# Retention ahead of two MLP layers on one core: output products grouped by tile shape, the last chunk widened to 128 tokens, and shared PSUM banks begun without zero products

## The chip, the cores and the metric

The kernel runs on one core of a Trainium2 chip. The metric is the device time in microseconds (us), here that of the one core. TensorE (PE in the profile) multiplies matrices into PSUM; VectorE (DVE), ScalarE (ACT) and GpSimd (POOL) work elementwise; SyncE (SP) issues most transfers. Each engine takes its instructions in a fixed order, so an instruction that waits holds up all that stand behind it on its engine.

## The reference

Retention (causal linear attention with a decay per head) is followed by two MLP layers. There are 4 batches, 8 heads, 576 tokens and 64 dimensions per head; the layers see 2304 tokens of 512 features and have 2048 hidden features.

```python
scores = scale * np.matmul(q, k.transpose(0, 1, 3, 2))
Dmat = np.where(rel >= 0, gamma[:, None, None] ** rel[None, :, :], 0.0)   # rel = i - j
attn_out = np.matmul(scores * Dmat, v)
x = attn_out.transpose(0, 2, 1, 3).reshape(2304, 512)
h = x @ moe_w_in;  x = np.maximum(0.01 * h, h) @ moe_w_out
h = x @ moe2_w_in; out = (h - np.tanh(h)) @ moe2_w_out
```

## The kernel before, in words

`retention()` goes through 16 pairs of heads (batch b, pair p), one pair per turn of its loop. The 576 tokens of a pair are four chunks of 128 (`NFULL`) and a last one of 64 (`TAIL`). Per pair the loop makes, in plain float32:

- `scores`: within each whole chunk, keys against queries (L393, one product per head and chunk, 64 rows of the array each), and the last chunk for both heads at once (L396, 64 stationary columns);
- `mask`: the causal mask and a decay factor on DVE (L406 for the whole chunks, L412 for the last), giving `pt`;
- `states_mm` and `states`: keys against values of each chunk (L424), from which ACT (L435) and DVE (L439) build the running state `st` at each chunk's end;
- `outputs_mm`, one pair later: for each chunk a "far" product of the state with the queries (L453, the full 128x128 array) and two "near" products of `pt` with the values (L458, 64 stationary columns for each head, in two halves of the array; for the last chunk 64 rows and 64 columns);
- `finish`: the outputs are split into a high part `xh` (ACT, L468) and a low part `xl` (DVE, L469), the last chunk first.

The queries and the values of the whole chunks are decayed in `prep` on POOL (L359, L364) one pair ahead, those of the last chunk in `prep_tail` on DVE (L372) and ACT (L382; L376 lays out its queries by head). Five transfers per pair are issued two pairs ahead by SP: queries, keys, `kn`, `vn`, and `vt` (the last chunk's values); each waits until the buffer it fills, one of three, is free.

From pair 5 on, each turn of the loop also has one step (the last turn two) of the first layer with 256 tokens: `h_mm` (L183, into `x_b`, 12 products of 256 columns in float32r, three for each of four slices, high and low parts), `act_a` and `chain` (L195, L217, L226, L227), and two steps later `o_mm` (L258, 12 products, into `a`). In the turns of pairs 0 to 8, DVE, ACT and POOL also turn the first weights from float64 bits into two float32r parts (`narrow_ops`, L126 to L147, and `split_piece`, L163 and L164); `fill` deals these steps out between the others. Where two outputs of 256 columns share a PSUM bank (`pack` is 2), `o_mm` first clears the bank with a product of one row of zeros (L243), 512 columns wide, and all others accumulate. This happens in six blocks: three in `retention`, and the block of 256 tokens of each of the other three groups of layer 1.

`layers()` does the rest of the two layers in steps of 512 tokens. The order on every engine is that in which the code is written (`manual_schedule`). The last chunk's scores `t_sc` and its output `o_tail` share the PSUM bank `x_a`; the far product into `o_tail` therefore stands behind the masking of `t_sc` (L412) of the pair that follows it.

Of the kernel before, what the change touches and what calls it, by code (L numbers as in the profile page):

```python
# [10 lines left out]
F32 = mybir.dt.float32  # L11
# [7 lines left out]
P = 128  # L19
CH = 128  # L20

# h - tanh(h) = tanh(h) * u * rho(u) with u = h^2 and rho(u) = (h / tanh(h) - 1) / u.
# For |h| <= TANH_T, rho(u) is RHO_C * (u - RHO_V)^2 + RHO_A to float32's accuracy.
# [4 lines left out]
# The float32 range, as the high words of float64 seen as float32.  # L28
# [5 lines left out]
def retention_moe_moe(  # L34
# [6 lines left out]
    vt: bass.AP,  # L41
# [32 lines left out]
    zero = keep.tile([P, 1], F32R, name="zero")  # L74

# [1 line left out]
    # Layer 1's first group takes QW tokens at a time while retention goes on.  # L77
# [33 lines left out]
    def narrow_ops(key):  # L111
        """The steps that make a float32 tile of a loaded piece."""
# [119 lines left out]
    def o_mm(s):  # L232
# [4 lines left out]
        if f == 0:  # L237
            ac_ps[s] = [
                pools["a"].tile([P, 512], F32, tag="a", name="a") for _ in range(cnt // pack)
            ]  # L240
            if pack > 1:
                for a in ac_ps[s]:
                    nc.tensor.matmul(  # L243
                        out=a, lhsT=zero[:1].to_broadcast([1, P]),
                        rhs=zero[:1].to_broadcast([1, 512]), start=True, stop=False,
                    )
        ps = ac_ps[s - f]
        gt, w = ga.pop(s), wt[m, 1, g * GF + f]
        for d in range(cnt):
# [3 lines left out]
            for i, (wi, gi) in enumerate(((0, 0), (0, 1), (1, 0))):  # L253
                if m == 0:
                    l, r = w[:, wi, ds], gt[:, gi, :n]
                else:
                    l, r = gt[:, gi, ds], w[:, wi, :]
                nc.tensor.matmul(  # L258
                    out=o, lhsT=l, rhs=r,
                    start=f == 0 and i == 0 and pack == 1,  # L260
                    stop=f == GF - 1 and i == 2 and (d + 1) % pack == 0,
                )
# [31 lines left out]
    def split_order(keys):  # L294
        """Pieces in the order in which the last block of a group lets go of their places."""
        return sorted(keys, key=lambda k: (k[2] + LAG * k[1], k[1]))

    def piece_ops(keys, split=True):
        """What the pieces take, in order: each is loaded two pieces ahead and split after
        the next one's first half."""  # L300
# [10 lines left out]
    def retention():  # L311
        with ExitStack() as ac:
# [8 lines left out]
            # The last chunk's scores of both heads and its output share a bank.  # L321
            x_a = ps_s.tile([P, 512], F32, name="x_a")
            x_b = ps_s.tile([P, 512], F32, name="x_b")
            t_sc = x_a[:TAIL, :2 * TAIL].rearrange("p (h r) -> p h r", h=2)
# [355 lines left out]
```

## Time and profile before

| | |
|---|---|
| median of 3 runs | 937.0 us (934.05 to 937.63) |
| span of the profiled execution | 935.3 us |
| median less that span | 1.7 us |
| PE busy | 906.2 us (97% of the span) |
| DVE, POOL, ACT busy | 595.9, 464.3, 397.6 us |

The profile is of one execution; no device time is listed for it beside its span, so the median is compared with the span. A busy PE is not a PE at its peak, because matmuls overlap: what a product costs is read from the start of one group to the start of the next. In the rows below a tile shape such as 128*64 is rows by columns of the array that a product uses. A float32 product has two entries, a float32r product one.

### The profile page before, as it was taken

Reading aid. Unit: us, or ns where it says so; the run is one execution under the profiler, and the core shown is the slowest. Engines: PE = TensorE matmul, PEld = TensorE weight load, DVE = VectorE, ACT = ScalarE, POOL = GpSimd, SP = SyncE. Lnnn points to the kernel's source line nnn. Section 1 sums busy time; section 2 is a strip of 40 time slices with the busy share of each in tenths; the row PEclk is TensorE's granted clock in tenths of the full one; section 3 lists DMA queues with packets and bytes.
Section 4 is the critical chain, followed back from the end, with each engine's and each line's share of the span. In section 5 each row is a group of like instructions: output and inputs, shape, how many; then the busy total and the mean of one; then the engine's idle time right before and its main releaser. Section 6 shows DMA issues by size and latency. Waiting matters only on the chain.

```text
span 935.3 us, 12947 instructions
## 1 busy us (share of the span) xinstructions
PE 906.2 (97%) x4844; PEld 737.5 (79%) x4844; DVE 595.9 (64%) x989; ACT 397.6 (43%) x809; POOL 464.3 (50%) x364
## 2 busy tenths in 40 slices
PE   4989999999999999999999999999999999999998
PEld 3667778888888888888888878888878877888886
DVE  5787554875555465527683677758886778754544
ACT  2443332224222322232333655576456545575454
POOL 3454421236222533245565855586457755595444
PEclk8999999999999999999999999999999999999999
DMA  7654340211111011101111011201120011001111
GB/s 233 224 178 154 103 141 13 78 68 46 46 68 46 0 46 68 68 1 46 46 52 39 3 46 66 69 1 45 46 68 23 23 45 68 1 1 46 45 46 68
DMA packets 22942, 57.78 MB, mean 62 GB/s; under 512 B 2784, under 2 KB 4192, under 8 KB 22880
## 3 DMA queue, kind: packets, MB, share of 16 engines
q1 hardware_dynamic: 22304, 56.63, 17.6%
q8 instruction: 38, 0.62, 0.3%
q10 hardware_dynamic: 576, 0.33, 0.1%
q14 instruction: 24, 0.20, 0.1%
HBM read 52.24 MB, written 4.72 MB: 61 GB/s over the span
## 4 chain that ended last, share of the span: by engine, by line
PE 70%; DVE 12%; POOL 9%; issue 4%; ACT 3%; DMA 2%; ACTq 0%; SPq 0%; DVEq 0%; POOLq 0%
PE a L258 32%; PE h L183 31%; POOL v L205 4%; POOL g L227 3%; DVE v L221 3%; DVE v L224 2%; DVE acc L282 2%; ACT g L226 2%; PE o L458 1%; PE x_b L183 1%; PE o L453 1%; DMA kv<-in_vt 1%; POOL wp L164 1%; PE sc L393 1%; DVE pt L406 1%
## 5 line engine op out<-in xcount | busy, mean ns | idle before, releaser
L183 PE MATMUL h<-xh,wp 128*128 128x512 f32 (+1 forms) x1216 | 374.7, 373 | 0.0
L183 PEld LDWEIGHTS h<-xh,wp 128*128 128x128 f32 x1216 | 222.0, 188 | 45.4
L183 PE MATMUL h<-xl,wp 128*128 128x512 f32 (+1 forms) x608 | 226.9, 373 | 0.0
L258 PE MATMUL a<-wp,g 128*128 128x512 f32 x864 | 212.9, 392 | 5.5 <-POOL g L227 5.3
L258 PE MATMUL a<-g,wp 128*128 128x512 f32 (+1 forms) x1008 | 214.2, 362 | 1.2 <-POOL g L227 1.2
L227 POOL TENSOR_TENSOR g<-a,g 128x512 fp32r<-128x512 f32 (+1 forms) x84 | 107.8, 1283 | 206.1 <-ACT g L226 194.7
L258 PEld LDWEIGHTS a<-g,wp 128*128 128x128 f32 x1008 | 171.4, 189 | 33.9 <-POOL g L227 1.4
L258 PEld LDWEIGHTS a<-wp,g 128*128 128x128 f32 x864 | 160.6, 188 | 43.9 <-POOL g L227 9.6
L227 POOL TENSOR_TENSOR g<-v,g 128x512 fp32r<-128x512 f32 (+1 forms) x80 | 103.9, 1298 | 142.1 <-ACT g L226 142.0
L183 PEld LDWEIGHTS h<-xl,wp 128*128 128x128 f32 x608 | 113.9, 187 | 22.6
L164 POOL TENSOR_TENSOR wp<-cw,wp 128x512 fp32r<-128x512 f32 x64 | 90.2, 1419 | 54.1 <-ACT wp L163 50.6
L147 DVE SCALAR_TENSOR_TENSOR cw<-st,cw 128x512 uint32<-128x512 uint32 x128 | 115.0, 898 | 3.0
L226 ACT ACTIVATE g<-v 128x512 fp32r<-128x512 f32 (+1 forms) x80 | 47.2, 590 | 163.4 <-DVE v L224 162.3
L195 ACT ACTIVATE a<-h 128x512 f32<-128x512 f32 (+1 forms) x72 | 40.5, 563 | 171.2 <-PE h L183 171.2
L217 DVE TENSOR_TENSOR a<-h,a 128x512 f32<-128x512 f32 (+1 forms) x72 | 46.3, 643 | 100.7 <-ACT a L195 100.6
L205 POOL TENSOR_TENSOR v<-t,u 128x512 f32<-128x512 f32 (+1 forms) x80 | 101.8, 1272 | 12.0 <-ACT t L204 11.9
L282 DVE TENSOR_TENSOR acc<-a,acc 128x512 f32<-128x512 f32 (+1 forms) x114 | 72.0, 659 | 51.5 <-PE a L258 51.5
L221 DVE SCALAR_TENSOR_TENSOR v<-q,v 128x512 f32<-128x512 f32 (+1 forms) x80 | 58.2, 728 | 59.1 <-POOL v L205 58.1
L220 DVE TENSOR_TENSOR h<-h,t 128x512 f32<-128x512 f32 (+1 forms) x80 | 51.2, 640 | 48.5 <-ACT t L204 48.5
L226 ACT ACTIVATE g<-a 128x512 fp32r<-128x512 f32 (+1 forms) x84 | 47.9, 570 | 80.2 <-DVE a L217 80.1
L141 DVE TENSOR_SCALAR cw<-cw 128x512 uint32<-128x512 uint32 x64 | 63.2, 988 | 1.5
L224 DVE COPY_PREDICATED v<-mk,h 128x512 f32<-128x512 uint32 (+1 forms) x80 | 54.9, 687 | 8.2
(60 smaller groups left out, 769.7 us busy)
## 6 DMA issues: line engine op xcount, KB each, us to landing
st<-in_w1i SPq DMA_DIRECT2D x16, 512.0 KB, 3.3
st<-in_w1o SPq DMA_DIRECT2D x16, 512.0 KB, 3.2
st<-in_w2i SPq DMA_DIRECT2D x16, 512.0 KB, 3.2
st<-in_w2o SPq DMA_DIRECT2D x16, 512.0 KB, 3.2
qk<-in_qT SPq DMA_DIRECT2D x16, 288.0 KB, 2.8
qk<-in_kT SPq DMA_DIRECT2D x16, 288.0 KB, 3.4
out<-acc SPq DMA_DIRECT2D x18, 256.0 KB, 2.1
kv<-in_kn SPq DMA_DIRECT2D x16, 256.0 KB, 4.2
```

What stands on the lines that cost most here:

```text
L141: nc.vector.tensor_scalar(out=t["w"], in0=t["w"], scalar1=3, scalar2=0x3FFFFFF8, op0=ALU.logical_shift_left, op1=ALU.bitwise_and,)
L147: nc.vector.scalar_tensor_tensor(out=t["w"], in0=t[src], scalar=scalar, in1=t["w"], op0=op, op1=ALU.bitwise_or)
L164: nc.gpsimd.tensor_tensor(out=wp[:, 1, :], in0=wf, in1=wp[:, 0, :].bitcast(F32), op=ALU.subtract)
L183: nc.tensor.matmul(out=ps[:, :n], lhsT=w[:, wi, cs], rhs=x[:, kk, t0:t0 + n], start=kk == 0 and i == 0, stop=kk == KK - 1 and i == 2,)
L205: nc.gpsimd.tensor_tensor(out=v[:, :n], in0=t_[:, :n], in1=u[:, :n], op=ALU.mult)
L220: nc.vector.tensor_tensor(out=h, in0=h, in1=t_, op=ALU.subtract)
L221: nc.vector.scalar_tensor_tensor(out=v, in0=q, scalar=RHO_A, in1=v, op0=ALU.add, op1=ALU.mult)
L224: nc.vector.copy_predicated(out=v, mask=mk.bitcast(U32), data=h)
L226: nc.scalar.activation(out=gt[:, 0, :n], in_=v, func=AF.Copy)
L227: nc.gpsimd.tensor_tensor(out=gt[:, 1, :n], in0=v, in1=gt[:, 0, :n].bitcast(F32), op=ALU.subtract)
L258: nc.tensor.matmul(out=o, lhsT=l, rhs=r, start=f == 0 and i == 0 and pack == 1, stop=f == GF - 1 and i == 2 and (d + 1) % pack == 0,)
L282: nc.vector.tensor_tensor(out=dst, in0=a, in1=dst, op=ALU.add)
```

## The change

Three things are changed. The far products of a pair are issued together (`outputs_far`), right behind the scores and the layer's `h_mm`, and its near products together (`outputs_near`), behind the layer's `o_mm`; the layer's `evac` moves ahead of `finish`, which takes the whole chunks first. The last chunk's stationary operands become 128 tokens (the last 128 of the pair, of which the first 64 have their values and their mask zeroed), so that its score and near products have the tile shapes 128*128 and 128*64; its values come with `vn` (no `vt`, one transfer less per pair), and are decayed in POOL's `prep`, so that L382 on ACT goes. Shared banks are cleared by the first product that writes into them, with its start flag, and the zero products go.

```diff
@@ -238,12 +236,6 @@
             ac_ps[s] = [
                 pools["a"].tile([P, 512], F32, tag="a", name="a") for _ in range(cnt // pack)
             ]
-            if pack > 1:
-                for a in ac_ps[s]:
-                    nc.tensor.matmul(
-                        out=a, lhsT=zero[:1].to_broadcast([1, P]),
-                        rhs=zero[:1].to_broadcast([1, 512]), start=True, stop=False,
-                    )
         ps = ac_ps[s - f]
         gt, w = ga.pop(s), wt[m, 1, g * GF + f]
         for d in range(cnt):
@@ -255,10 +247,12 @@
                     l, r = w[:, wi, ds], gt[:, gi, :n]
                 else:
                     l, r = gt[:, gi, ds], w[:, wi, :]
+
                 nc.tensor.matmul(
                     out=o, lhsT=l, rhs=r,
-                    start=f == 0 and i == 0 and pack == 1,
+                    start=f == 0 and i == 0 and d % pack == 0,
                     stop=f == GF - 1 and i == 2 and (d + 1) % pack == 0,
+                    skip_group_check=pack > 1,
                 )
 
     def evac(s):
...
-            t_sc = x_a[:TAIL, :2 * TAIL].rearrange("p (h r) -> p h r", h=2)
+            t_sc = x_a[:, :2 * TAIL].rearrange("p (h r) -> p h r", h=2)
...
-            cm_sb = ak.tile([P, 1, CH], F32, name="cm_sb")
+            cm_sb = ak.tile([P, 1, CH + TAIL], F32, name="cm_sb")
-            vt_sb = ak.tile([P, NP, 1, 2, 1], F32, name="vt_sb")
+            vt_sb = ak.tile([P, NP, NCH, 2, 1], F32, name="vt_sb")
...
             def load_v(i):
                 b, p = order[i]
-                t = ap_.tile([P, 2 * NFULL + 1, P], F32, tag="kv", name="kv")
+                t = ap_.tile([P, NFULL + NCH, P], F32, tag="kv", name="kv")
                 nc.sync.dma_start(out=t[:, :NFULL, :], in_=kn[b, p])
-                nc.sync.dma_start(out=t[:, NFULL:2 * NFULL, :], in_=vn[b, p])
-                nc.sync.dma_start(out=t[:TAIL, 2 * NFULL, :], in_=vt[b, p])
+                nc.sync.dma_start(out=t[:, NFULL:, :], in_=vn[b, p])
                 kv[i] = t
...
-                v = kv[i][:, NFULL:2 * NFULL, :].rearrange("p c (h d) -> p c h d", h=2)
+                v = kv[i][:, NFULL:, :].rearrange("p c (h d) -> p c h d", h=2)
                 nc.gpsimd.tensor_tensor(
-                    out=v, in0=v, in1=vt_sb[:, p].to_broadcast([P, NFULL, 2, P // 2]), op=ALU.mult
+                    out=v, in0=v, in1=vt_sb[:, p].to_broadcast([P, NCH, 2, P // 2]), op=ALU.mult
...
-                for h in range(2):
-                    o = slice(64 * h, 64 * h + 64)
-                    v = kv[i][:TAIL, 2 * NFULL, o]
-                    nc.scalar.activation(
-                        out=v, in_=v, func=AF.Copy, scale=vt_sb[:TAIL, p, 0, h, :]
-                    )
...
+                return sc
+
+            def scores_tail(i):
                 nc.tensor.matmul(
-                    out=t_sc, lhsT=kt[:, MAIN:], rhs=bds[i % 2], start=True, stop=True
-                )
-                return sc
+                    out=t_sc, lhsT=qk[i][:, 0, S - CH:], rhs=bds[i % 2], start=True, stop=True
+                )
...
-                        in1=cm_sb.to_broadcast([P, NFULL, CH]), op0=ALU.mult, op1=ALU.mult,
+                        in1=cm_sb[:, :, :CH].to_broadcast([P, NFULL, CH]),
+                        op0=ALU.mult, op1=ALU.mult,
                 for h in range(2):
                     nc.vector.scalar_tensor_tensor(
-                        out=pt[:TAIL, h, MAIN:], in0=t_sc[:, h, :], scalar=back[h],
-                        in1=cm_sb[:TAIL, 0, :TAIL], op0=ALU.mult, op1=ALU.mult,
+                        out=pt[:, h, MAIN:], in0=t_sc[:, h, :], scalar=back[h],
+                        in1=cm_sb[:, 0, CH:], op0=ALU.mult, op1=ALU.mult,
...
-            def outputs_mm(i):
-                pt, q, st, t = pts.pop(i), qk.pop(i)[:, 1, :], sts[i % 2], kv.pop(i)
+            def chunk_out(o_, c):
+                n = min(CH, S - c * CH)
+                cs = slice(c * CH, c * CH + n)
+                return (o_[:, cs] if c < NFULL else o_tail), cs
+
+            def outputs_far(i):
+                q, st = qk.pop(i)[:, 1, :], sts[i % 2]
                 o_ = ps_s.tile([P, 512], F32, tag="o", name="o")
+                for c in range(1, NCH):
+                    dst, cs = chunk_out(o_, c)
+                    nc.tensor.matmul(
+                        out=dst, lhsT=st[:, c - 1, :], rhs=q[:, cs],
+                        start=c in (1, NFULL), stop=False, skip_group_check=True,
+                    )
+                return o_
+
+            def outputs_near(i, o_):
+                pt, t = pts.pop(i), kv.pop(i)
                 for c in range(NCH):
-                    n = min(CH, S - c * CH)
-                    cs = slice(c * CH, c * CH + n)
-                    dst = o_[:, cs] if c < NFULL else o_tail
-                    if c:
-                        nc.tensor.matmul(
-                            out=dst, lhsT=st[:, c - 1, :], rhs=q[:, cs], start=True, stop=False
-                        )
+                    dst, cs = chunk_out(o_, c)
                     for h in range(2):
                         o = slice(64 * h, 64 * h + 64)
                         nc.tensor.matmul(
-                            out=dst[o], lhsT=t[:n, NFULL + c, o], rhs=pt[:n, h, cs],
-                            start=c == 0, stop=True,
+                            out=dst[o], lhsT=t[:, NFULL + c, o], rhs=pt[:, h, cs],
+                            start=False, stop=True, skip_group_check=True,
                         )
-                return o_
...
-                for src, lo, hi in ((o_tail, MAIN, S), (ot, 0, MAIN)):
+                for src, lo, hi in ((ot, 0, MAIN), (o_tail, MAIN, S)):
...
                 sc = scores(i)
+                scores_tail(i)
                 mask(i, sc)
                 if i + 1 < len(order):
...
                     h_mm(s)
                     act_a(s)
                 fill(i, 0)
+                if i:
+                    ot = outputs_far(i - 1)
                 if n_steps:
                     chain(s)
                     fill(i, 1)
-                if i:
-                    ot = outputs_mm(i - 1)
                 if s >= LAG:
                     o_mm(s - LAG)
+                if i:
+                    outputs_near(i - 1, ot)
                 states_mm(i)
+                if s >= LAG:
+                    evac(s - LAG)
                 if i:
                     finish(i - 1, ot)
-                if s >= LAG:
-                    evac(s - LAG)
                 fill(i, 1)
                 states(i)
                 fill(i, 2)
...
             last = len(order) - 1
             chain(s - 1)
-            ot = outputs_mm(last)
+            ot = outputs_far(last)
             o_mm(s - 2)
+            outputs_near(last, ot)
             finish(last, ot)
             evac(s - 2)
             o_mm(s - 1)
             evac(s - 1)
...
+    back = gamma ** -r[:, None].astype(float)
+    tail = S - S // CH * CH
+    late = np.concatenate([np.zeros((CH - tail, H)), back[:tail]])
+    late_mask = np.concatenate([np.zeros((CH - tail, tail)), rel[:tail, :tail] >= 0])
+    vtab = np.stack([back] * (S // CH) + [late], axis=1)
...
```

PE's order in a steady pair, before: from the last `h_mm` product (x_b) of one turn to the scores of the next. In the names, o and x_a are a pair's outputs, a the layer's, c the states' products, sc the scores.

```order
L183 MATMUL x_b<-xh,wp 128x256
L458 MATMUL o<-pt,kv 64x128 x2
L453 MATMUL o<-qk,st_98 128x128
L458 MATMUL o<-pt,kv 64x128 x2
L453 MATMUL o<-qk,st_98 128x128
L458 MATMUL o<-pt,kv 64x128 x2
L453 MATMUL o<-qk,st_98 128x128
L458 MATMUL o<-pt,kv 64x128 x2
L453 MATMUL x_a<-qk,st_98 128x64
L458 MATMUL x_a<-pt,kv 64x64 x2
L258 MATMUL a<-g,wp 128x256 x12
L424 MATMUL c<-kv 64x64 x8
```

The same place in PE's order after the change, with the scores that follow (L447 is the far product, L459 the near one, L251 the layer's, L415 the states', L381 and L387 the scores).

```order
L181 MATMUL x_b<-xh,wp 128x256
L447 MATMUL o<-qk,st_97 128x128 x3
L447 MATMUL x_a<-qk,st_97 128x64
L251 MATMUL a<-g,wp 128x256 x12
L459 MATMUL o<-pt,kv 64x128 x8
L459 MATMUL x_a<-pt,kv 64x64 x2
L415 MATMUL c<-kv 64x64 x8
L381 MATMUL sc<-qk 128x128 x8
L387 MATMUL x_a<-bd_99,qk 128x128
```

The far product into x_a, which stands behind the mask of the next pair's last chunk, moves from ninth to fourth place after the scores' work, and the near products move behind the layer's twelve.

DVE's order in a steady pair, before: from one pair's states to the next.

```order
L439 SCALAR_TENSOR_TENSOR st_97<-st_97,c 64x64 x6
L406 SCALAR_TENSOR_TENSOR pt<-sc,cm_sb 128x512 x2
L412 SCALAR_TENSOR_TENSOR pt<-x_a,cm_sb 64x64 x2
L372 TENSOR_TENSOR qk<-qk,qt_sb 128x64
L217 TENSOR_TENSOR a<-x_b,a 128x256
L469 TENSOR_TENSOR xl<-x_a,xh 128x64
L469 TENSOR_TENSOR xl<-o,xh 128x512
L439 SCALAR_TENSOR_TENSOR st_98<-st_98,c 64x64 x6
```

And after the change.

```order
L430 SCALAR_TENSOR_TENSOR st_97<-st_97,c 64x64 x6
L396 SCALAR_TENSOR_TENSOR pt<-sc,cm_sb 128x512 x2
L403 SCALAR_TENSOR_TENSOR pt<-x_a,cm_sb 128x64 x2
L366 TENSOR_TENSOR qk<-qk,qt_sb 128x64
L215 TENSOR_TENSOR a<-x_b,a 128x256
L469 TENSOR_TENSOR xl<-o,xh 128x512
L469 TENSOR_TENSOR xl<-x_a,xh 128x64
L430 SCALAR_TENSOR_TENSOR st_96<-st_96,c 64x64 x6
```

On DVE only the two subtractions of `finish` change places; the order of states, masks and subtractions stays, while on PE the products they wait for moved.

## Rows read from the trace of the kernel before

**Rows 1.** The page, busy time and share of the span by engine.

```profile
PE 906.2 (97%) x4844; PEld 737.5 (79%) x4844; DVE 595.9 (64%) x989; ACT 397.6 (43%) x809; POOL 464.3 (50%) x364
```

**Rows 2.** Busy time by stretch: PE, PEld, DVE, ACT, POOL, PEclk, DMA share, GB/s.

```profile
75.04:85.39 10.35, 9.91 (x97) 7.49 (x96) 8.93 (x19) 3.94 (x12) 5.54 (x5) 1.00 0.34 114
85.39:93.28 7.89, 6.29 (x56) 5.52 (x57) 4.33 (x15) 3.57 (x11) 1.50 (x2) 0.78 0.45 147
112.23:120.83 8.60, 8.60 (x88) 6.79 (x90) 4.75 (x15) 2.94 (x10) 3.05 (x3) 1.00 0.42 134
...
260.00:935.00 675.00, 664.83 (x3094) 546.15 (x3092) 427.92 (x631) 309.08 (x581) 366.50 (x281) 1.00 0.12 41
```

**Rows 3.** The chain that ended last, one pair: start us, us, what.

```profile
109.20 1.09 PE sc L393 x16
110.65 1.57 PE x_b L183 x12
112.23 0.37 PE o L458 x4
112.60 0.42 PE o L453 x2
...
115.59 1.60 PE a L258 x12
117.19 0.61 PE c L424 x16
```

**Rows 4.** The same chain in the layers, around zero products.

```profile
268.64 0.63 PE a L243 x2
269.26 1.62 PE a L258 x12
270.88 1.38 PE h L183 x12
272.26 1.42 PE a L258 x12
```

**Rows 5.** DVE's instructions in order of time: start, us, operation, tiles, idle before.

```profile
85.39 1.29 DVE L406 SCALAR_TENSOR_TENSOR pt<-sc,cm_sb 128x512 f32<-128x512 f32 x2
...
116.54 0.69 DVE L469 TENSOR_TENSOR xl<-o,xh 128x512 fp32r<-128x512 f32 x1 [0.26 <-ACT xh L468]
118.40 1.45 DVE L439 SCALAR_TENSOR_TENSOR st<-st,c 64x64 f32<-64x64 f32 x6 [1.17 <-ACT st L435]
119.86 1.29 DVE L406 SCALAR_TENSOR_TENSOR pt<-sc,cm_sb 128x512 f32<-128x512 f32 x2
121.07 0.34 DVE L412 SCALAR_TENSOR_TENSOR pt<-x_a,cm_sb 64x64 f32<-64x64 f32 x2
...
137.19 1.29 DVE L406 SCALAR_TENSOR_TENSOR pt<-sc,cm_sb 128x512 f32<-128x512 f32 x2
```

**Rows 6.** ACT's instructions in order of time, the split of one pair's outputs.

```profile
115.92 0.59 ACT L468 ACTIVATE xh<-o 128x512 fp32r<-128x512 f32 x1
```

**Rows 7.** A pair with weight narrowing: DVE and POOL in order of time.

```profile
78.33 0.42 DVE L217 TENSOR_TENSOR a<-x_b,a 128x256 f32<-128x256 f32 x1 [1.02 <-ACT a L195]
82.49 2.89 DVE L147 SCALAR_TENSOR_TENSOR cw<-st,cw 128x512 uint32<-128x512 uint32 x2
83.39 1.45 POOL L364 TENSOR_TENSOR kv<-kv,vt_sb 128x512 f32<-128x512 f32 x1
```

**Rows 8.** Waits up to 150 us (us in total, times, longest), and the chain's start.

```profile
ACT kv L382 <- DMA kv<-in_vt: 8.5, 4, 3.9
...
7.52 5.90 DMA kv<-in_vt
```

**Rows 9.** PE in order of time and the chain, behind a long wait.

```profile
86.99 0.43 PE L453 MATMUL x_a<-qk,st 128*128 128x64 f32 x2 [1.68 <-DVE pt L412]
...
87.69 2.53 PE a L258 x12
```

**Rows 10.** Groups by line up to 210 us: busy, mean ns, idle before: weight loads.

```profile
L183 PEld LDWEIGHTS x_b<-xh,wp 128*128 128x128 f32 x96 | 15.4, 188 | 2.0 <-issue 1.9
```

More of the change, by code (lines that the diff above doesn't have):

```diff
@@ L40, in retention_moe_moe @@
     vn: bass.AP,
-    vt: bass.AP,
     w1i: bass.AP,
@@ L73, in retention_moe_moe @@
     qb = keep.tile([P, 4], F32, name="qb")
-    zero = keep.tile([P, 1], F32R, name="zero")
     QW, EARLY = 256, 3
@@ L499, in retention @@
             nc.vector.memset(qb[:, 2:3], 0.0)
-            nc.vector.tensor_copy(out=zero, in_=qb[:, 2:3])
             nc.vector.memset(qb[:, 0:1], -RHO_V * math.sqrt(RHO_C))
@@ L632, in heads_t, with tokens @@
         return np.ascontiguousarray(a.transpose(0, 1, 3, 2)).reshape(B, NP, 2 * D, S)
-    def tokens(a):
+    def tokens(a, last):
         a = a.reshape(B, NP, 2, S, D).transpose(0, 1, 3, 2, 4).reshape(B, NP, S, 2 * D)
         main = S // CH * CH
-        head = a[:, :, :main].reshape(B, NP, main // CH, CH, 2 * D).transpose(0, 1, 3, 2, 4)
-        return np.ascontiguousarray(head), np.ascontiguousarray(a[:, :, main:])
+        chunks = a[:, :, :main].reshape(B, NP, main // CH, CH, 2 * D)
+        if last:
+            chunks = np.concatenate([chunks, a[:, :, None, S - CH:]], axis=2)
+        return np.ascontiguousarray(chunks.transpose(0, 1, 3, 2, 4))
     def bits(w):
@@ L656 @@
     row_gamma = np.repeat(gamma.reshape(NP, 2), D, axis=1).T
+    back = gamma ** -r[:, None].astype(float)
[3 more added lines that the diff above has]
+    vtab = np.stack([back] * (S // CH) + [late], axis=1)
     consts = {
-        "cmask": (rel >= 0)[:, None, :],
+        "cmask": np.concatenate([rel >= 0, late_mask], axis=1)[:, None, :],
         "qtab": row_gamma[:, :, None] ** (CH + r) * scale,
-        "vtab": (gamma ** -r[:, None].astype(float)).reshape(CH, NP, 1, 2, 1),
+        "vtab": vtab.reshape(CH, -1, NP, 2).transpose(0, 2, 1, 3)[..., None],
     }
-    (kn, _), (vn, vt) = tokens(k), tokens(v)
     arrays = {
-        "qT": heads_t(q), "kT": heads_t(k), "kn": kn, "vn": vn, "vt": vt,
+        "qT": heads_t(q), "kT": heads_t(k), "kn": tokens(k, False), "vn": tokens(v, True),
         "w1i": w_in(inputs["moe_w_in"]), "w1o": w_out(inputs["moe_w_out"]),
```

## The prediction

> **What bounds the kernel now.** I read the busy shares first [rows 1]: PE is at 97%, no other engine above 64%. That is an average over stages, so next the busy time by stretch [rows 2]. From 260 us on PE works 664.83 of 675 us: the layers are bound by PE, and time taken from its products there is time gained. So is the second part of retention: in the stretch of one pair from 112.23 to 120.83 us PE is busy all of 8.60 us, DVE 4.75. The first part is not. From 75.04 to 85.39 DVE is busy 8.93 of 10.35 us, and from 85.39 PE idles and is granted a clock of 0.78. So a gain on PE counts in full in the layers, in the pairs from 9 on only until the next limit, and hardly in the pairs before.
>
> The chain of waits shows what a steady pair costs on PE [rows 3]: 8.60 us from one `scores` to the end of the next states (109.20 to 117.19 + 0.61). In it a pair of near products and a far product take turns, 0.37 and 0.42 us.
>
> **A change of tile shape.** Three pairs of rows price it. The 12 products of `h_mm` take 1.57 us behind the last chunk's scores, which use half the array's columns [rows 3], and 1.38 in the layers behind full-array products [rows 4]. The 12 of `o_mm` take 1.60 us behind near products [rows 3] and 1.62 behind zero products, but 1.42 behind full-array ones [rows 4]. Each difference is 0.18 to 0.20 us for one change of shape: 0.19.
>
> **Grouping, on PE.** From one `scores` to the next the order before changes shape 14 times: into the scores, the last chunk's score, `h_mm`, the first near products, then eight changes along far and near, `o_mm` and the states. After it: into the scores, into the last chunk's score (now the full array, as are `h_mm`, far products and `o_mm`), into the near products (the shape of the states, which follow). Eleven fewer, 2.1 us, leave 6.5. This checks: 14 x 0.19 leaves 5.94 us of streaming, and a far product less one change is 0.42 - 0.19 = 0.23, a near pair 0.18 to 0.21. The last chunk's operands of 128 tokens stream as many columns as before and cost PE nothing; DVE's masks of 128 instead of 64 partitions have the same number of elements per partition, so I leave them at 0.34 for two.
>
> **What is late next.** The near products now stand behind `o_mm`, so what follows them is no longer hidden by it. Count from N, the end of the near products. ACT starts on the whole chunks' `xh` 0.33 us later now (115.59 to 115.92), behind the last chunk's; first in line I take 0.2, and it takes 0.59 [rows 3, 6]. DVE's `xl` starts 0.03 later and takes 0.69; its instructions overlap by some 0.07 (121.07 is 0.08 before 119.86 + 1.29), so 0.62 goes to it, 0.15 to the last chunk's, 1.45 to the states, 1.21 and 0.34 to the masks [rows 5]. That is N + 4.6, and the far product into `x_a` waits for it. PE comes there at N + 0.4 (states, no change of shape) + 1.1 + 0.4 + 1.4 + 0.7 = N + 4.0, so it waits about 0.6 us; queued behind it are `o_mm`, the near products, and so DVE's next subtractions. From the mask: 0.06 to start, 0.11 for the far product of 64 columns, 1.42 for `o_mm`, 1.1 for ten near products (four pairs of 0.2, one of half that, one change). The loop closes at 4.6 + 2.7 = 7.3, less 0.1 because the whole chunks end before the last: 7.2 to 7.3, I take 7.25. Ends: 6.5, if PE stays the bound, and 8.6, if grouping saves nothing.
>
> **The terms.**
> Pairs 9 to 15: the masks of pair 9 start at 85.39, those of pair 15 at 137.19 [rows 5], 51.8 us for six periods; 6 x 7.25 = 43.5. Minus 8.3 (this includes the zero products of one block).
> The end of retention: from the last scores to the first step of the layers the order has 25 changes of shape before and 5 after, 3.8 us, and two zero products less, which stream 0.63 - 0.19 = 0.44; one wait for the masks takes back 0.6. Minus 3.6.
> The layers: a block with zero products costs 0.63 and a slower `o_mm` (1.62 against 1.42) [rows 4], 0.83; three blocks. Minus 2.5.
> The start: the chain begins with `vt`, which lands after 5.90 us [rows 8]; ACT's L382 waits for it, and the weights' first step on ACT, DVE's narrowing and the masks of pair 1 stand behind it. L382 waited 8.5 us in four waits. The transfer goes, but `vn` grows by a quarter, and the weight piece behind it lands at about the same time, so of 5.9 us I take 1.5; in the next turns, where L382 holds up `xh`, 1.5 more. Minus 3.0, between 0 and 6.
> Pairs 5 to 8, bound by DVE: in some L382's 0.6 us goes out of DVE's wait (1.02 before L217) [rows 7]. Against it POOL's L364 grows from 512 to 640 elements, by a quarter of the 1.45 us in the row at most, 0.36. While POOL runs, DVE's narrowing waits: two L147 took 2.89 us across L364 [rows 7], so up to 0.36 us more in about three of the pairs. And `xl` waits for PE's 0.06 + 0.11 + 1.42 + 1.1 + 0.8 = 3.5 us behind the masks, in the place of which DVE now has narrowing steps of its own. I take 0.
> SP issues one transfer less per pair, and queries are released earlier, by the far products; nothing on the path waits for either in a steady pair.
>
> Sum: 8.3 + 3.6 + 2.5 + 3.0 = 17.4 us off the span of 935.3: 917.9. The median was 1.7 above the span: 919.6 us.
>
> **Rivals.**
> *PE's clock falls in the first part (925.6).* There PE will have 2 us less work in pairs that DVE bounds, and will stand in one piece at the far product into `x_a`. A wait of 1.68 us at that place now is followed by `o_mm` at 2.53 us instead of 1.60 [rows 9, 3], and by the granted clock of 0.78 over the pair [rows 2]: half clock for part of it. If four of pairs 5 to 9 get such a fall more, with 1.5 us each, 6 us go. Against it: one such fall, at pair 9, is in the time already, and an `o_mm` that waits for nothing follows. The Trainium skill, "TensorE: Matmul & The Clock Gate", section "HAM oscillation — how this bites in real kernels", describes kernels that fall back to half clock in each turn of a loop because of gaps between bursts of matmuls; by that rule, this rival.
> *It goes throughout and the kernel gets slower (943).* At half clock `o_mm` takes 2.5, the near products 2.1, the far product 0.2: the loop is 4.6 + 4.9 = 9.5 us against 8.60 now, plus 5.2 us over six pairs; pairs 5 to 8 lose 2 us each, 8; the end of retention (3.6), the layers (2.5) and half of the start (1.5) still gain: plus 5.6, 943. It decides from about 0.8 us per pair over ten pairs, which eats the 7.6 us of the other terms. Against it: in a steady pair PE waits only 0.6 us of 7.25.
> *Grouping saves nothing (931).* If what I call a change of shape is a weight load that a neighbour in the same rows cannot hide, a run of four far products costs what four single ones do, 0.42 each. Then only the zero products (2.5 in the layers, 2 x 0.63 in retention's later part), and about 2.5 of the start are gained: 6 us. Against it: the 12 products of 256 columns come every 0.115 us (1.38 / 12) while one weight load takes 0.188 [rows 4, 10], so loads do hide among full-array products of float32r; for float32 no row shows such a run. The Trainium skill, the same page, section "Part 3: Packing small matmuls — row/col tiling", says that a weight load overlaps matmuls in flight only when its row group differs, which speaks for this rival; the row just named does not bear it out.
> *PE stays the bound (912).* If DVE and ACT run earlier than I count, the loop is 6.5 us: 4.5 us more in six pairs, and 3 more at the start.
>
> **How the numbers follow.** My forecast 0.62, the clock in the first part 0.14, nothing from grouping 0.10, PE the bound 0.08, slower throughout 0.06. The time is that of the first, 919.6. The range of 911 to 928 takes in the second and fourth and leaves out 0.16; its ends come from the loop's 6.5 to some 8, and the start's 0 to 6. 0.5% is 4.7 us, about what a measurement of this kernel can tell from no change. Faster: the first, second and fourth, and half of the third, 0.89; same, the other half, 0.05; slower 0.06.
>
> **What would show it.** Right: `o_mm` at about 1.42 us behind the far products; far products at about 0.23 each, ten near products at about 1.1; a steady pair at 7.2 us with a wait of about half a us of the far product into `x_a` for the mask; no L243 and 0.83 us less around each block of 256 tokens in the layers; the masks of pair 9 some 3 us earlier. Wrong: a pair still at 8.6; a half clock behind the waits in pairs 5 to 8 or in the steady pairs; or POOL's longer `prep` showing in DVE's narrowing, with the masks of pair 9 later than 85.39.

## The result and the profile after

Over four runs each on one chip the changed kernel took 927.41 us (925.63 to 930.78) and the kernel before 936.66 (934.05 to 937.63): a ratio of 0.9904, 95% interval 0.9875 to 0.9933. It is faster by 1%, inside the range on record and 7.8 us above the forecast. The profiled execution took 927.96 us, its span is 926.1: 9.2 us less than before, where 17.4 were forecast.

The page of the changed kernel answers to [rows 1]; its last line here is the granted clock in 40 slices:

```profile
span 926.1 us, 12850 instructions
PE 886.5 (96%) x4832; PEld 739.7 (80%) x4832; DVE 597.6 (65%) x988; ACT 388.0 (42%) x777; POOL 468.5 (51%) x364
PEclk9989999999999999999999999999999999999999
```

PE has 19.7 us less busy time, and the span fell by less than half of that: the rest has turned into waits. To see where, I cut the span at three places of which each trace has a row: the start of DVE's masks of pair 9, those of pair 15, and PE's first `h_mm` of the layers. Times in us, of the profiled executions:

| kernel | masks of pair 9 start at | pairs 9 to 15 | to the layers | layers to the end | span |
|---|---|---|---|---|---|
| before | 85.39 | 51.80 | 16.26 | 781.85 | 935.3 |
| after | 85.03 | 45.34 | 13.08 | 782.65 | 926.1 |
| forecast of the difference | -3.0 | -8.3 | -3.6 | -2.5 | -17.4 |
| measured | -0.4 | -6.5 | -3.2 | +0.8 | -9.2 |

The two terms in the middle came nearly as forecast, the first and the last not at all.

**A steady pair.** PE in order of time in the changed kernel (start us, us, operation, tiles, and in brackets the idle time before and its releaser); it answers to [rows 3]:

```profile
108.39 0.83 PE L447 MATMUL o<-qk,st 128*128 128x128 f32 x6
109.51 0.43 PE L447 MATMUL x_a<-qk,st 128*128 128x64 f32 x2 [0.30 <-DVE pt L403]
109.76 1.67 PE L251 MATMUL a<-g,wp 128*128 128x256 f32 x12
111.35 1.09 PE L459 MATMUL o<-pt,kv 128*64 128x128 f32 x16
112.28 0.28 PE L459 MATMUL x_a<-pt,kv 128*64 128x64 f32 x4
112.39 0.64 PE L415 MATMUL c<-kv 128*64 128x64 f32 x16
112.96 1.16 PE L381 MATMUL sc<-qk 64*128 64x128 f32 x16
114.05 0.49 PE L387 MATMUL x_a<-bd,qk 128*128 128x128 f32 x2
114.30 0.36 PE L181 MATMUL x_b<-xh,wp 128*128 128x256 f32 x1
...
115.79 0.83 PE L447 MATMUL o<-qk,st 128*128 128x128 f32 x6
116.92 0.44 PE L447 MATMUL x_a<-qk,st 128*128 128x64 f32 x2 [0.30 <-DVE pt L403]
```

From start to start a pair takes 7.40 us (115.79 less 108.39), against 8.60. Ten near products take 1.04 us (111.35 to 112.39). What the far products cost can't be read here, because the wait for the mask stands behind them; without that wait three of them take 0.67 us, some 0.22 each (e5 below, 100.86 to 101.53). The wait for the mask stands where it was forecast, with 0.30 us.

**A pair bound by DVE.** PE and then DVE in pair 8 of the changed kernel, columns as above; they answer to [rows 7, 9]:

```profile
75.24 0.67 PE L447 MATMUL x_a<-qk,st 128*128 128x64 f32 x2 [2.51 <-DVE pt L403]
75.67 2.91 PE L251 MATMUL a<-g,wp 128*128 128x256 f32 x12
78.51 1.17 PE L459 MATMUL o<-pt,kv 128*64 128x128 f32 x16
```

```profile
74.84 0.34 DVE L403 SCALAR_TENSOR_TENSOR pt<-x_a,cm_sb 128x64 f32<-128x64 f32 x2
...
77.50 0.97 DVE L139 TENSOR_SCALAR cw<-cw 128x512 uint32<-128x512 uint32 x1
80.36 0.69 DVE L469 TENSOR_TENSOR xl<-o,xh 128x512 fp32r<-128x512 f32 x1 [1.89 <-ACT xh L468]
...
85.03 1.29 DVE L396 SCALAR_TENSOR_TENSOR pt<-sc,cm_sb 128x512 f32<-128x512 f32 x2
```

PE stands 2.51 us for the mask of 74.84, then needs 2.84 us (75.67 to 78.51) for an `o_mm` of 1.6, and DVE, out of narrowing steps, stands 1.89 us for the near products behind it. The waits from 40 to 92 us (us in total, times, longest) say how often:

```profile
PE x_a L447 <- DVE pt L403: 11.5, 4, 3.3
...
DVE xl L469 <- ACT xh L468: 6.9, 5, 2.1
```

In the same stretch of the kernel before, the far product waited 4.8 us in five waits and `xl` 1.5 in five. Busy time by stretch of the changed kernel (PE, PEld, DVE, ACT, POOL, PEclk, DMA share, GB/s), as in [rows 2]:

```profile
40.00:92.00 52.00, 39.03 (x437) 36.20 (x432) 40.48 (x97) 18.98 (x55) 26.31 (x22) 0.90 0.53 172
75.20:78.60 3.40, 3.36 (x16) 3.14 (x18) 2.54 (x5) 1.89 (x5) 0.73 (x1) 0.51 0.47 141
107.91:115.31 7.40, 7.10 (x88) 6.59 (x87) 4.86 (x14) 2.39 (x8) 3.21 (x3) 1.00 0.49 156
260.00:935.00 675.00, 655.23 (x3027) 539.21 (x3025) 422.44 (x621) 306.95 (x576) 364.72 (x279) 1.00 0.12 40
464.30:467.70 3.40, 3.40 (x15) 3.08 (x14) 3.33 (x5) 0.47 (x2) 1.72 (x2) 0.52 0.42 154
```

Behind the wait of 2.51 us the granted clock is 0.51, about the lower of its levels (1.2 of 2.4 GHz); in the steady pair, with its waits of 0.30 us, it is 1.00. The last line is in the layers, at a wait for POOL:

```profile
463.93 2.33 PE L251 MATMUL a<-g,wp 128*128 128x256 f32 x11 [1.90 <-POOL g L225]
466.06 0.63 PE L181 MATMUL h<-xh,wp 128*128 128x512 f32 x1
```

### The profile page after: what moved, and what is told of

Read it like the earlier page. It is cut to its first block, busy times and chain, and to the rows that moved or that the text cites. A ratio compares the mean times of both kernels' runs of the same rounds, so it can differ in the third digit from the quotient of the medians.

```text
span 926.1 us, 12850 instructions
## 1 busy us (share of the span) xinstructions
PE 886.5 (96%) x4832; PEld 739.7 (80%) x4832; DVE 597.6 (65%) x988; ACT 388.0 (42%) x777; POOL 468.5 (51%) x364
## 4 chain that ended last, share of the span: by engine, by line
PE 60%; DVE 17%; POOL 11%; issue 6%; ACT 5%; DMA 1%; DVEq 0%; POOLq 0%; ACTq 0%
PE a L251 29%; PE h L181 28%; POOL v L203 5%; POOL g L225 4%; DVE v L219 4%; DVE v L222 3%; ACT g L224 2%; DVE acc L276 2%; DVE st L430 2%; DVE pt L396 2%; PE o L459 2%; POOL wp L162 1%; DVE cw L139 1%; ACT xh L468 1%; DVE cw L134 1%
## 5 line engine op out<-in xcount | busy, mean ns | idle before, releaser
L251 PE MATMUL a<-wp,g 128*128 128x512 f32 x864 | 213.4, 393 | 5.2 <-POOL g L225 5.0
L251 PE MATMUL a<-g,wp 128*128 128x512 f32 (+1 forms) x1008 | 216.3, 364 | 1.9 <-POOL g L225 1.9
L251 PEld LDWEIGHTS a<-g,wp 128*128 128x128 f32 x1008 | 173.6, 192 | 32.3 <-POOL g L225 2.1
L251 PEld LDWEIGHTS a<-wp,g 128*128 128x128 f32 x864 | 160.9, 188 | 43.8 <-POOL g L225 9.2
```

The lines of the kernel that those rows point to most:

```text
L251: nc.tensor.matmul(out=o, lhsT=l, rhs=r, start=f == 0 and i == 0 and d % pack == 0, stop=f == GF - 1 and i == 2 and (d + 1) % pack == 0, s ...
```

## The experiments

The theory: the changed order puts the near products behind a far product that waits for DVE's mask and behind `o_mm`; where DVE is the bound (pairs 5 to 9) DVE waits for them in turn, with PE at half clock behind its own wait, and that eats what the rest of the change gains at the start. The rivals: the wider last chunk (POOL's longer `prep`), the start that never came earlier, or the zero products. Times are medians beside the kernel before on the same chip (937.27 us for the first four, 938.11 for the next four, 938.25 for the last four), with the ratio and its 95% interval; the segments are those of the table above. The segments come from one execution each. e7 has the code of the changed kernel up to the layers, and e10 that of e5, and yet their masks of pair 9 start 0.9 and 0.8 us later: a difference of under 1 us there shows nothing.

| kernel | masks of pair 9 start at | pairs 9 to 15 | to the layers | layers to the end | median, ratio |
|---|---|---|---|---|---|
| e1_group_only | 92.04 | 47.64 | 14.17 | 781.65 | 936.6, 0.9985 (0.9971 to 1.0) |
| e2_no_zero_only | 84.94 | 51.21 | 15.65 | 780.10 | 934.04, 0.9968 (0.9951 to 0.9986) |
| e3_widen_only | 82.82 | 49.86 | 16.23 | 781.79 | 931.3, 0.9927 (0.9903 to 0.995) |
| e4_zero_back | 87.91 | 47.68 | 13.81 | 781.90 | 932.64, 0.9945 (0.9927 to 0.9964) |
| e5_own_bank | 79.26 | 42.60 | 12.45 | 782.69 | 918.67, 0.9791 (0.9762 to 0.9821) |
| e6_omm_late | 81.48 | 43.85 | 12.99 | 781.48 | 922.97, 0.984 (0.9811 to 0.9869) |
| e7_zero_last | 85.95 | 45.55 | 13.08 | 780.32 | 926.8, 0.9881 (0.9856 to 0.9905) |
| e8_filler | 83.27 | 45.10 | 13.08 | 781.05 | 925.11, 0.986 (0.9837 to 0.9884) |
| e10_own_zero_last | 80.04 | 42.57 | 12.45 | 780.34 | 916.7, 0.9768 (0.9745 to 0.9791) |
| e11_own_late_zero_last | 78.99 | 43.61 | 12.37 | 780.43 | 918.58, 0.9788 (0.9765 to 0.9812) |
| e12_own_ungrouped | 96.02 | 49.05 | 15.46 | 781.67 | 939.07, 1.0004 (0.9984 to 1.0025) |
| e14_change_ungrouped | 79.30 | 49.26 | 15.59 | 781.75 | 927.61, 0.9885 (0.9863 to 0.9906) |

### e1_group_only: the kernel before, with the order of the products alone

`outputs_mm` keeps the far products, the near ones go to `outputs_near`; the turn of the loop becomes that of the changed kernel.

```diff
...
+                if i:
+                    ot = outputs_mm(i - 1)
                 if n_steps:
                     chain(s)
                     fill(i, 1)
-                if i:
-                    ot = outputs_mm(i - 1)
                 if s >= LAG:
                     o_mm(s - LAG)
+                if i:
+                    outputs_near(i - 1, ot)
                 states_mm(i)
...
```

> Grouping alone: far and near products apart as in the change, with the last chunk's 64-token operands, its vt transfer, L382 and the zero products as before. If a change of shape costs 0.19 us and the loop through the masks is what is left: steady pairs at about 7.45 us as in the change, the end of retention 2.5 us shorter, pairs 0 to 8 within 1.5 us of before, the layers as before; in all 928 to 930. If the gain comes from the widened chunk or the missing zero products: about 936.

I expected a gain, and there is none that can be measured: 936.6. The steady pairs and the end give 4.2 and 2.1 us, and the masks of pair 9 come 6.65 us later. PE, then DVE, then busy time by stretch, in and around pair 7:

```profile
70.09 0.69 PE L450 MATMUL x_a<-qk,st 128*128 128x64 f32 x2 [1.86 <-DVE pt L412]
70.71 1.22 PE L243 MATMUL a<-zero 1*128 1x512 f32 x2
71.86 2.93 PE L258 MATMUL a<-g,wp 128*128 128x256 f32 x12
74.72 1.80 PE L467 MATMUL o<-pt,kv 128*64 128x128 f32 x16
```

```profile
77.20 0.69 DVE L477 TENSOR_TENSOR xl<-o,xh 128x512 fp32r<-128x512 f32 x1 [3.45 <-ACT xh L476]
```

```profile
65.90:76.10 10.20, 8.34 (x42) 7.05 (x42) 6.41 (x11) 2.46 (x7) 3.01 (x3) 0.50 0.25 86
```

Everything that PE does there ahead of the near products, zero products too, runs at half clock, and DVE stands 3.45 us. This is the theory's chain at its longest, and it comes without the wider chunk.

### e2_no_zero_only: the kernel before without its zero products

```diff
-            if pack > 1:
-                for a in ac_ps[s]:
-                    nc.tensor.matmul(
...
-                    start=f == 0 and i == 0 and pack == 1,
+                    start=f == 0 and i == 0 and d % pack == 0,
...
```

> The zero products alone taken out of the kernel before. By my first sum 0.83 us for each of six blocks, 5 us: 932. If the third block of the layers only turns its share into a wait for POOL, with a fall of PE's clock behind it (which the changed kernel showed at 464 us): two blocks of the layers and two of retention gain 0.7 to 0.8 each, the third loses up to 1.6: 934 to 936.

It gains 3 us, 1.75 of them in the layers.

### e3_widen_only: the wider last chunk alone

The changed kernel with the zero products and with the old order of the products, of `finish` and of the copies in it.

```diff
...
-                if i:
-                    ot = outputs_far(i - 1)
                 if n_steps:
                     chain(s)
                     fill(i, 1)
+                if i:
+                    ot = outputs_mm(i - 1)
                 if s >= LAG:
                     o_mm(s - LAG)
-                if i:
-                    outputs_near(i - 1, ot)
                 states_mm(i)
...
```

> The widened last chunk alone (no vt, no L382, POOL's prep of 640 elements, one change of shape less per pair); order and zero products as before. If the start gains from vt and L382 and POOL's longer prep is hidden: masks of pair 9 two to three us earlier, steady pairs 8.4 us: 932 to 934. If POOL's longer prep is what ate the start in the changed kernel: masks of pair 9 at 85.4 us or later, 936 to 938.

It gains 6 us by the median; of 4.6 us in the span, 2.6 lie ahead of pair 9 and 1.9 in the pairs after it. The wider chunk, with POOL's longer `prep`, is no loss.

### e4_zero_back: the changed kernel with its zero products back

```diff
+            if pack > 1:
+                for a in ac_ps[s]:
+                    nc.tensor.matmul(
+                        out=a, lhsT=zero[:1].to_broadcast([1, P]),
+                        rhs=zero[:1].to_broadcast([1, 512]), start=True, stop=False,
+                    )
...
```

> The changed kernel with its zero products put back. By the first sum 0.83 us for each block more: 931 to 932. If the zero products' place in the third block is only a wait, and their absence costs PE its clock there: two blocks of the layers +1.5, retention +1.2, the third block -1.6 to -2: 928 to 929, and no half clock near 464 us.

Without this part the change is worth 4.6 us, not 9: one block's zero products stand ahead of the near products in turns that are late already (87.91 against 85.03, and against 85.95 in e7), one block costs in pairs 9 to 15 and one at the end (2.3 and 0.7 us). e4 and e3 differ by grouping alone, both with the zero products: with it the masks of pair 9 start 5.1 us later (87.91 against 82.82).

### e5_own_bank: the last chunk's scores out of the outputs' bank

They move from `x_a` into the free half of the states' bank, and are issued behind `h_mm`, so that the far product into `x_a` waits for no mask. No run has one of the two edits without the other.

```diff
-            t_sc = x_a[:, :2 * TAIL].rearrange("p (h r) -> p h r", h=2)
+            x_c = ps_s.tile([P, 512], F32, name="x_c")
+            t_sc = x_c[:, QW:QW + 2 * TAIL].rearrange("p (h r) -> p h r", h=2)
...
-                c_ = ps_s.tile([P, NFULL, 64], F32, tag="c", name="c")
+                c_ = x_c[:, :NFULL * 64].rearrange("p (c d) -> p c d", c=NFULL)
...
```

> The changed kernel with the last chunk's score moved from the bank of its output to the unused half of the states' bank (and issued behind h_mm), so that the far product waits for no mask. If the loop far product, o_mm, near products, finish, states, masks is what holds steady pairs at 7.45 us: they fall to PE's own 6.5 to 6.7, the DVE-bound pairs lose DVE's waits for the high parts (1.8 to 2.1 us in pairs 7 to 9), in all 917 to 921. If something else holds them (DVE, POOL, transfers): 926 to 928.

918.67, and a ratio of 0.9791 where the change alone had 0.9904. PE in order of time in a steady pair, then the busy time from 40 to 92 us:

```profile
100.63 0.39 PE L388 MATMUL x_c<-bd,qk 128*128 128x128 f32 x2
100.86 0.83 PE L448 MATMUL o<-qk,st 128*128 128x128 f32 x6
101.53 0.33 PE L448 MATMUL x_a<-qk,st 128*128 128x64 f32 x2
101.67 1.66 PE L251 MATMUL a<-g,wp 128*128 128x256 f32 x12
103.25 1.09 PE L460 MATMUL o<-pt,kv 128*64 128x128 f32 x16
...
104.29 0.64 PE L416 MATMUL x_c<-kv 128*64 128x64 f32 x16
104.86 1.16 PE L382 MATMUL sc<-qk 64*128 64x128 f32 x16
```

```profile
40.00:92.00 52.00, 40.32 (x494) 36.99 (x493) 43.84 (x105) 19.60 (x60) 29.92 (x25) 1.00 0.56 183
```

The far product waits for nothing, and the six periods from pair 9 to 15 take 7.1 us on average, more than the 6.5 to 6.7 that I expected. In the DVE-bound stretch PE still waits (9.3 us in six waits, now for DVE's states ahead of the last chunk's score), but its clock stays at 1.00, `xl` waits 2.3 us instead of 6.9, and DVE gets 3.4 us more done (43.84 against 40.48).

### e6_omm_late: `o_mm` behind the near products and the states

```diff
-                if s >= LAG:
-                    o_mm(s - LAG)
                 if i:
                     outputs_near(i - 1, ot)
                 states_mm(i)
                 if s >= LAG:
-                    evac(s - LAG)
+                    o_mm(s - LAG)
                 if i:
                     finish(i - 1, ot)
+                if s >= LAG:
+                    evac(s - LAG)
```

The layer's `evac`, which copies what `o_mm` made, goes behind `finish` with it.

> The changed kernel with the layer's o_mm moved behind the near products and the states' products, as cover for finish; one change of shape more per pair. If o_mm ahead of the near products is what lengthens the loop: it falls to 4.6 + 1.3 = 5.9 us, PE becomes the bound at 6.7, and in pairs 7 to 9 the 1.4 us that o_mm takes goes out of DVE's wait: 918 to 921. If not: 927 or more.

Its 922.97 us lie between the two times that I expected. It gains 3.55 us by pair 9 with the wait for the mask still there (8.5 us in four waits, `xl` 1.3): what stands between the mask and the near products has a price of its own.

### e7_zero_last: zero products in the last group alone

```diff
+            if pack > 1 and g == NG - 1:
+                for a in ac_ps[s]:
...
```

> The changed kernel with the two zero products put back only in the last group's block of 256 tokens, where PE waits for POOL. If their absence lets PE idle 1.9 us and its clock fall for 3.4 us there: the wait is 1.2 us or less, no half clock near 464 us, 1.5 to 2 us less than the changed kernel, 925.5 to 926. If the fall has another cause: a half clock again there, and the same time or 0.8 us more.

The layers take 780.32 us, 2.3 less than in the changed kernel; the median moves by less than the interval can tell. Of the 2.3 some 0.9 belong to another effect (see the account of the layers below). PE at the place of the wait for POOL shown above:

```profile
464.62 1.58 PE L258 MATMUL a<-g,wp 128*128 128x256 f32 x11 [1.14 <-POOL g L226]
466.04 0.40 PE L182 MATMUL h<-xh,wp 128*128 128x512 f32 x1
```

Here the wait is 0.76 us shorter, as long as the zero products ran ahead of it, and what follows it is at full speed.

### e8_filler: work in the place of the wait

For the outputs of pairs 4, 6, 7 and 8 the whole chunks' far products are issued five times over, so that PE has work while the mask is on its way.

```diff
+            FILL = {4: 4, 6: 4, 7: 4, 8: 4}
+
...
-                for c in range(1, NCH):
+                again = FILL.get(i, 0) * list(range(1, NFULL))
+                for c in again + list(range(1, NCH)):
```

> The changed kernel with the three whole-chunk far products issued five times instead of once in four of the DVE-bound pairs (those that finish pairs 4, 6, 7 and 8), so that PE works 2.6 us in the place where it would wait for the mask. The results are the same. If half clock behind these waits costs time: no half clock at 48 to 51, 65 to 68 and 75 to 78.6 us, o_mm 1.6 us instead of 2.2 and 2.8, masks of pair 9 two to three us earlier, 924 to 926. If the waits alone are the cost: no change or slightly slower, 927 to 929.

PE in order of time in pair 8, and the busy time from 40 to 92 us:

```profile
75.22 1.67 PE L251 MATMUL a<-g,wp 128*128 128x256 f32 x12
```

```profile
40.00:92.00 52.00, 48.42 (x564) 45.76 (x562) 43.12 (x102) 19.42 (x55) 27.36 (x22) 0.99 0.55 178
```

With more work PE is earlier: the clock stays at 0.99, `o_mm` takes 1.67 us instead of 2.91, and the masks of pair 9 come 1.76 us sooner. The masks of pair 5, ahead of which nothing was changed, start 1.03 us later here (46.18 against 45.15), so from there to pair 9 it gains 2.8. Some 1.8 to 2.8 us are thus the part of the half clock. DVE still waits 4.0 us for `xl`.

### e10_own_zero_last and e11_own_late_zero_last: the parts that paid, together

e10 is e5 and e7, e11 is e10 with the order of e6; no further edits.

> The changed kernel with the last chunk's score in the states' bank, and the two zero products of the last group's block of 256 tokens put back. If the two effects are independent: retention as with the own bank alone (masks of pair 9 near 79.3 us, steady pairs 7.1 us), the layers 780.3 us instead of 782.7 and no half clock near 455 us: 915.5 to 917. If the fall near 455 has another cause: 918 to 919.

> The same, and o_mm behind the near and the states' products as well. If finish behind o_mm is still a wait once no product waits for a mask: pairs 7 to 9 gain up to 1 us each, 913 to 916. If the mask's wait was what made it one: the change of shape more that this order has costs 0.2 us in nine pairs, 916 to 918.

e10 is the fastest kernel of this study: 916.7 us. The layers take 780.34 us, 2.35 less than in e5, though the intervals of e5 and e10 overlap. `o_mm` behind the states adds nothing once no product waits for the mask: it gains 1 us by pair 9, hardly more than the 0.8 by which e5 and e10 differ there, and loses 1 in the pairs after it.

### e12_own_ungrouped and e14_change_ungrouped: the change without grouping

e14 is the changed kernel in the old order (the edit of e3, without its zero products); e12 is e14 with the bank of e5. Both have the tile `zero` in memory, though nothing uses it.

> The changed kernel without its grouping: widened chunk and no zero products, far and near products in the order of before. If the grouping of the change is worth nothing in all, because pairs 0 to 8 give back what the steady pairs gain: masks of pair 9 near 82.5 us, steady pairs 8.2 to 8.3, 927 to 930, the time of the changed kernel within 0.3%. If grouping is worth 1.2 us in each steady pair and nothing is given back: 935 or more.

> The changed kernel with the last chunk's score in the states' bank, but far and near products in the order of before (widened chunk, no zero products). If grouping is worth 0.19 us per change of shape once PE is the bound: steady pairs at 8.2 to 8.4 us instead of 7.1, 926 to 929. If the bank alone made the gain: 918 to 921.

e14 cannot be told from the changed kernel (0.9885 and 0.9904, the intervals overlap). Its masks of pair 9 start at 79.30, 5.7 us sooner; its pairs 9 to 15 and the end take 3.9 and 2.5 us more. So grouping as it was placed gives 6.4 us and takes 5.7; the other 0.9 is in the layers (782.65 against 781.75). With the bank of e5 grouping takes nothing ahead of pair 9: 79.26 there, as in e14. e12 shows that the bank alone does nothing for steady pairs (49.05 us, 8.2 each): it is grouping that the bank sets free. Neither of the times that I expected of e12 came, because its start went wrong; PE in order of time and busy time by stretch:

```profile
11.68 1.06 PE L383 MATMUL sc<-qk 64*128 64x128 f32 x8
16.69 0.77 PE L389 MATMUL x_c<-bd,qk 128*128 128x128 f32 x2 [3.95 <-DVE st L432]
```

```profile
16.30:57.30 41.00, 38.91 (x255) 28.11 (x256) 21.16 (x64) 9.75 (x29) 14.03 (x12) 0.50 0.42 141
57.30:96.00 38.70, 34.97 (x351) 27.16 (x349) 35.04 (x75) 13.80 (x40) 21.89 (x18) 1.00 0.52 180
```

PE is granted half clock for 41 us, though it is busy for 38.91 of them, and by pair 9 this execution has lost 16.7 us to e14 (96.02 against 79.30). The wait of 3.95 us didn't start it: the scores ahead of it take 1.06 us for eight entries, where a steady pair takes 1.16 for sixteen. The first scores of all 14 kernels are as slow (2.08 us for sixteen at some 5.5 us), in a stretch that the trace gives as 1.00; in the 13 others they are down to 1.16 by 31.6 us at the latest, in e12 only behind 57. This execution is the slowest of ten (943.97 us), and the other nine have no trace. Four of them took 936.93 to 940.32 us with a mean clock of 1.000 on record. As the record misses the slow start, it can't tell whether they were slow in the same way. Nothing was tried that explains it.

## Why the forecast came out this way

The time lies inside the range, 0.6 us below its upper end, and that is in part luck: of 17.4 us only 9.2 came. The range allowed for a start that gains nothing and for a loop of 8 us. Neither of these happened; a gain at the start was lost again in pairs that were put at nothing.

**The start (-3.0) and pairs 5 to 8 (0): the second is the step that failed.** The start was worth what was forecast: the masks of pair 5 start at 45.15 us, 48.50 before (44.36 in e3, with the wider chunk and the old order). No run parts the transfer of `vt` from ACT's L382. Then the gain is lost, to 2.9 us at pair 7, 1.4 at pair 8 and 0.4 at pair 9. The prediction put the time from the masks to `xl` at 3.5 us, and let narrowing steps of DVE's own fill that time. In pair 8 it is 5.2 us (75.18, the end of the masks, to 80.36): at half clock `o_mm` takes 1.2 us more, and the steps to fill it run out 1.89 us early. In pair 9, at full clock, it is 3.7 us (86.59 to 90.25). e14, without grouping, keeps the gain (79.30). What the runs show of its parts, which overlap and don't add: half clock behind the wait 1.8 to 2.8 us (e8), `o_mm` ahead of the near products 3.55 (e6), the wait for the mask with all that follows from it 5.8 (e5). So this is the rival of the falling clock in part only: that one priced the clock alone at 6 us, and the place of `o_mm` cost at least as much as the clock did. POOL's longer `prep` is not the cause: e3 and e14 have it, and their pair 9 is early. The Trainium skill, "TensorE: Matmul & The Clock Gate", section "HAM oscillation — how this bites in real kernels", says that gaps between bursts of matmuls bring the half clock back in each turn. The rows agree with it in part. Behind the waits for the mask in pairs 5, 7 and 8 the clock falls (2.51 us idle in pair 8, then 0.51). In the steady pairs it doesn't (0.30 us idle, 1.00), nor in pair 9, where the wait is longer than in pair 8 and `o_mm` takes 1.67 us behind it:

```profile
86.64 0.43 PE L447 MATMUL x_a<-qk,st 128*128 128x64 f32 x2 [2.78 <-DVE pt L403]
86.88 1.67 PE L251 MATMUL a<-g,wp 128*128 128x256 f32 x12
```

So the length of the wait alone does not decide; what does stays open.

**The steady pairs (-8.3; -6.5).** Right in mechanism: the loop through the masks is the bound, with the far product into `x_a` waiting in each pair. The loop is 7.40 us instead of 7.25 in a plain pair, and 8.06 and 7.64 in two of the six, in which DVE also copies a finished block (L274). PE's own part was mis-sized: forecast 6.5 us without waits, 6.84 in e5 (98.02 to 104.86, from one `scores` to the next). Of 8.60 us, 1.76 go for eleven changes of shape, 0.16 each instead of 0.19. `o_mm` is part of it: I put it at 1.42 us behind full-array products, and it takes 1.59 (109.76 to 111.35) ahead of near products, so the price of a change is seen ahead of it too. That grouping saves nothing on PE, one of the rivals, is refuted; that PE becomes the bound, another, is what e5 comes to, and not the change.

**The end of retention (-3.6; -3.2)** is right.

**The layers (-2.5; +0.8).** For two of three blocks the sum holds: e4 and e7 differ by their zero products and by 1.58 us, 0.79 a block, where 0.83 was forecast. The third block has a wait for POOL behind its first step. Before the change it was 1.16 us, and the zero products ran in the time that is now added to it: 1.90. So nothing is gained there, and in the changed kernel the half clock that follows (0.52 for 3.40 us) takes back 1.5 us: the eleven products of `o_mm` take 2.13 us (463.93 to 466.06) instead of 1.42, the `h_mm` behind them 3.60 instead of 2.81. Whether it comes differs from kernel to kernel. In e2 PE waits as long, and stays at full speed:

```profile
471.75 1.58 PE L252 MATMUL a<-g,wp 128*128 128x256 f32 x11 [1.95 <-POOL g L227]
473.17 0.40 PE L183 MATMUL h<-xh,wp 128*128 128x512 f32 x1
```

Of the 14 kernels profiled, seven have zero products there and none falls; of the seven without, four fall (after, e5, e12, e14) and three don't (e2, e6, e8). What decides it among these stays open. The sum, 781.85 less 1.58 plus 1.5, fits e12 and e14 (781.67 and 781.75); the changed kernel and e5 take some 0.9 us more (782.65 and 782.69). This is spread over the layers: from 500 to 900 us an `h_mm` product of 512 columns takes 396 ns on average in these two, and in e6 and e8, and 394 ns in each of the ten other kernels. What parts the four from the ten is the tile `zero` of one column, which the change took out of memory together with the zero products: e7 and e10 have it back, e12 and e14 have it without using it. So some 0.9 us of the layers' forecast go with that tile; why, no run shows.

## What to carry to other kernels

Before grouping a queue's products by kind, ask which of them waits for another engine: what stands behind it in the new order is then late for that engine too, and where that engine is the bound, the saved time is paid back (6.4 us gained, 5.7 lost here). Take the wait away first, here by another bank for a few scores; then grouping is worth some 1.1 us a pair (7.1 against 8.2). Cheap work ahead of a wait that comes anyway cost nothing here: taken out, it left a longer wait (1.90 us for 1.16), and in four kernels of seven half clock behind it.

## What was not expected of the hardware

More work made PE faster: with 48 far products more in the place of waits (e8: for four pairs, four times three) the masks of pair 9 came 1.76 us sooner. Waits of 1.90 to 1.95 us at the same place of the program were followed by half clock in four kernels and by full speed in three, and in the changed kernel a wait of 2.51 us was followed by half clock and one of 2.78 by full speed. In e12 half clock lasted for 41 us of nearly unbroken work (busy for 38.91), while e5, with PE busy for 31.30 us of the same stretch, was at full speed from its scores at 21.20 us on (1.29 us for sixteen entries, then 1.16). And the granted clock on record is not the whole story: at the start it reads 1.00 while the scores take 2.08 us.
